# Two attention blocks on one core: block A's work two pieces earlier, a second place for output groups in two late units, and four small moves

## The chip, the cores and the metric

The program runs on one core of a Trainium2 chip. The core has TensorE (PE in the profile; its weight loads are listed as PEld), VectorE (DVE), ScalarE (ACT), GpSimd (POOL) and SyncE (SP), which here only issues DMAs, in program order on one queue. The metric is device time in microseconds (us); lower is better. A measurement is the median of several runs, and one more execution was taken with the profiler.

## The reference

Two independent attention blocks, A and B, each on its own input of 2048 rows x 640 columns with 32 heads of 20 columns; all in float32.

```
qkv = x @ wqkv                      # [S, 3, H, Dh]
A:  logits[s, w] = q[s] . k[s - 2 w] * Dh**-0.5   for w = 0..7 (masked where s - 2 w < 0)
    o = softmax(logits) over w, times v[s - 2 w]
B:  scores = q k^T * Dh**-0.5 ;  o = softmax(scores) v     # all 2048 keys
out = concat(o_A @ wo_A, o_B @ wo_B)
```

So A is a sliding window of eight keys with a step of two, and B is full attention with 32 heads.

## The kernel before, in words

Every projection splits each float32 operand into a rounded high part and a low remainder ("split") and adds three products (`PASSES`): 15 matmuls per output tile of 128 rows. A copy makes the high part and a subtraction the low part; which engines do it is set per call in `split` (L175; ACT and DVE unless `first` and `second` say otherwise).

**Stage 1 (L525 to L577)** projects q, k and v of block A for its first 12 tiles of 128 rows and stores them to DRAM (`qa_d`, `ka_d`, `va_d`). **Stage 2 (L612 to L651)** projects q and k of block B: five values of `m`, four column blocks `n`, two halves `j`, that is 40 groups, each of 15 matmuls with 512 columns, in turn over all eight PSUM banks (`all_banks`). Each result is stored to `kb_d` (m = 0, 2 and half of 4) or `qb_d`. In its last row `m == 8` it also starts the loads for B's attention: `b_keys(0)` returns four DMAs for the k stack of the first four heads (L586), `b_queries` four for each of four query blocks (L594).

**Stage 3 (L1021 to L1055)** projects v of block B: 30 of 32 groups (`v_group`, 15 matmuls with 320 columns, results on four PSUM banks). Between them it computes the first 24 steps of row maxima, `b_max(i)` (L753): four q.k matmuls into two pairs of banks (`wide`, which alternates between the two pairs), each pair read by one VectorE reduction of 128 x 1024. One `b_max` follows each group from the seventh on.

**Stage 4, the loop (L1091)**, has 512 steps in 32 units of 16. Each unit holds the attention of four heads for 512 queries: per step four score matmuls with the keys on partitions (`ss` two at once, or `sm` one of them beside one matmul for the maxima), four exponentials on ACT, four matmuls with v (`b_pv`, marked `P`), and 24 steps ahead the matmuls for the row maxima (`MM` or `sm`), which VectorE reduces. The order of a unit is written out by hand in three lists: `UNIT_V` (L877) for units 0 to 23, `UNIT` (L873) for units 24 to 29, and `PAIR` for the half unit 30 until the maxima end. Beside these, `V` stands for one group of A's remaining projections (tiles 12 to 15, `a_more`, L1004), and `G` for one group of A's output projection (`group`, L1083), which also lets VectorE's small operations run that have been collected in `beside`. In the last 60 steps `G` takes two output groups if they are ready. A small planner (`one`, `two`, `b_two`) picks the PSUM bank for each matmul from estimated end times.

**Block A's attention** runs on GpSimd as 128 pieces (`UNITS`, L348): for each tile four pieces of keys and four of values, each of two window positions. `a_fetch` loads a piece two pieces ahead, `a_attention` (L450) is a generator, and each `next(a_work)` emits one piece: 12 times in stage 2 (L649), 8 times in stage 3, then every fourth step of the loop from step 15. The softmax of a tile starts with its fourth piece of keys; its small VectorE operations wait for the next `G`, unless the tile is in `late`, when they are emitted at once (L403). The last tile has no keys of a following tile between its own keys and its values. A finished tile is transposed (`a_turn`, five VectorE transposes at a `G`, then a round trip through DRAM), split by GpSimd into `aot`, of which there is one buffer (`turn_parts`, L496), and used by two output groups of 15 matmuls.

**The end.** From step 488 on, steps run in pairs without maxima. Output rows of B are normalised on GpSimd, stored to `ot_b`, loaded back and split (`out_first` for four chunks, `out_last` for the fifth, L927), and multiplied by `wo_b` in groups of 15 matmuls.

SP, GpSimd, PE, ACT and DVE all keep program order: what is emitted ahead of an instruction runs ahead of it on that engine. Nearly all instructions are recorded under one line (L61), so the profile is read by tile names: `ve` is a v projection, `bk,bq` and `bq,bk` are q.k matmuls for maxima and scores, `mx` the maxima, `e` the exponentials, `e,vb` the matmuls with v, `more` and `braw` B's partial sums, `akv`, `al`, `am` and `ao` block A's work, `xl` the fifth chunk of split rows, `ww` split weights.

Of the kernel before, what the change touches and what calls it, by code (L numbers as in the profile page):

```python
# [40 lines left out]
NKB = 16  # L41
# [24 lines left out]
def attention_pair(ctx, tc, xa, wqk_a, wv_a, wo_a, xb, wqk_b, wv_b, wo_b, oa, ob):  # L66
# [108 lines left out]
    def split(hi, lo, src, tag="stg", second=None, first=None):  # L175

        t = sb.tile([128, 640 if tag == "stg" else 1024], F32, tag=tag, bufs=3 if tag == "stg" else PB, name="stg")
        raw = t[:, :src.free_size()] if len(src.shape) == 2 else (
            t[:, :src.shape[1] * src.shape[2]].rearrange("p (k c) -> p k c", c=src.shape[2]))
        sp.dma_start(raw, src)  # L180

        def parts():
            (first or act.copy)(hi, raw)
            (second or dve).tensor_tensor(lo, raw, hi.bitcast(F32), ALU.subtract)
        after(odd(wait[0]), parts)
# [167 lines left out]
    def a_fetch(n):  # L353
        if n >= len(UNITS):
            return
        t, c = UNITS[n]
        assert loop[0] is None or t < in_dram[0]
        hf, r0 = divmod(t * 128, HS)
        if c == 0:
            q = sb.tile([128, D], F32, tag="aq", bufs=2, name="aq")  # L360
            sp.dma_start(q, qa_d[hf, r0:r0 + 128])
            a_t[t] = [q, None, None]
        kv = sb.tile([128, 2, D], F32, tag="akv", bufs=4, name="akv")
        src = ka_d if c < 4 else va_d
        for o in range(2):
            r = r0 + 2 * (c % 4) + o
            sp.dma_start(kv[:, o], src[hf, r:r + 128])
        a_kv[n] = kv
# [217 lines left out]
    def b_keys(g):  # L586
        k = big(3 * (g % 2), [128, 2, S], "bk")
        v = sb.tile([128, NKB, VG], F32, tag="vb", bufs=2, name="vb")
        stacks[g] = (k, v)
        return [lambda r=r, r0=r0, s0=s0, n=n: sp.dma_start(  # L590
            k[r * HALF + r0:r * HALF + r0 + n].bitcast(F32), kb_d[s0:s0 + n, g * GH + 2 * r:g * GH + 2 * r + 2])
            for r in range(2) for r0, s0, n in BK_RUNS]
# [20 lines left out]
    for m in range(0, 10, 2):  # L613
        nxt = []
        for n in range(4):
            for j in range(2):
                p = next(banks)
                for k in range(KC):
                    for i, (wi, xi) in enumerate(PASSES):
                        pe.matmul(p, WB[j][:, wi, k], chunk(XB[n], xi, k), start=(k == 0 and i == 0),  # L620
                                  stop=(k == KC - 1 and i == 2))
                c = MS[m + j]
                o = (0, 1) if c < KC else (1, 0)
                pt = sb.tile([128, 2, 512], F32R, tag="p", bufs=PB, name="pr")
                act.copy(pt[:, o[0]], p)
                dve.tensor_tensor(pt[:, o[1]], p, pt[:, o[0]].bitcast(F32), ALU.subtract)
                after(1, sp.dma_start, dst_b(c, n).rearrange("t p c -> p t c"), pt.bitcast(F32))
                tick()
                if loads:
                    loads.pop(0)()  # L630
                if m < 8 and (n, j) in ((1, 0), (1, 1)):
                    w, loads = m_pieces(MS[m + 2 + len(nxt)])
                    nxt.append(w)
                elif m == 8 and (n, j) == (0, 1):
                    WV, loads = wide_pieces(wv_b[0])
                elif m == 8 and n == 3:
                    if j == 0:
                        wait[0] = 4
                        w1, more = wide_pieces(wv_b[1])
                        for fn in more:  # L640
                            fn()
                if m == 8 and n > 1:
                    if (n, j) == (2, 0):
                        k_loads = b_keys(0)
                        rings.append(big(1, [128, NQC, 2, 512], "bq"))
                        q_loads = [fn for qc in range(NQC) for fn in b_queries(0, qc)]
                    k_loads.pop(0)()
                groups += 1
                if 4 < groups < 34 and groups * 2 % 5 < 2:  # L649
                    next(a_work, None)  # L650
        WB = nxt  # L651
    tick()
# [183 lines left out]
    def b_two(what):  # L836
# [41 lines left out]
        "sm P sm MM ss P sm ss MM sm P ss MM sm P sm sm MM sm V sm ss MM sm P sm MM ss P sm MM sm ss P sm MM "  # L878
        "ss P sm MM sm ss P sm sm sm P sm ss MM ss G sm MM ss sm P sm MM ss P sm MM sm ss P sm sm sm P sm ss "
        "MM sm P sm MM ss P sm MM ss").split()  # L880
    SLOT = UNIT[:UNIT.index("G")].count("P") - 1

    def b_units(pv, group, more):

        scores = ((i, pl, r) for i in range(NS - LEAD) for pl in range(2) for r in range(2))
        maxima = ((m, j) for m in range(LEAD, NS) for j in range(2))
        steps = iter(range(-LAG, NS))
        half = []
        for i in range(0, NS - LEAD, NKB):
            for t in UNIT_V if i // NKB < 6 * (NT - UP) else UNIT if i + NKB <= NS - LEAD else PAIR * (NKB // 4):  # L890
                if t == "P":
                    yield
                    pv(next(steps))
                elif t == "G":
                    group()
                elif t == "V":
                    more()
                elif t == "ss":
                    b_two([("s", *next(scores)) for _ in range(2)])
                elif t == "MM":  # L900
                    m, j = next(maxima)
                    max_tiles(m)
                    b_two([("m", m, j, r) for r in range(2)])
                    max_end(m, 1)
                else:
                    s = next(scores)
                    shut = bool(half)
                    m, j, r = half.pop() if shut else (*next(maxima), 1 - s[2])
                    max_tiles(m)
                    if not shut:  # L910
                        half.append((m, j, 1 - r))
                    b_two([("s", *s), ("m", m, j, r)])
                    if shut:
                        max_end(m, 1)
# [12 lines left out]
    def out_last(qc):  # L927
        o = outs_b[qc]
        k = KC - 1
        split(chunk(o, 0, k), chunk(o, 1, k), ot_b[k * 128:(k + 1) * 128, qc * 512:(qc + 1) * 512])  # L930
        if qc < NQC - 1:
            for n in range(8):
                after(3 + (1 + (qc < 2)) * n, fill.append, lambda n=n: out_group(qc, n))
# [42 lines left out]

    rows_a = [(t + j, m) for t in range(UP, NT, 2) for m in range(6) for j in range(2)]
    xt, wt = {}, []
    in_dram = [UP]

    def a_columns(t):

# [20 lines left out]

    def a_more():  # L1004

        t, m = rows_a.pop(0)
        x, w = xt[t], wt[0]
        p = bank()
        rows15(p, lambda xi, k: chunk(x, xi, k), [w[:, 0], w[:, 1]])
        hf, r0 = divmod(t * 128, HS)  # L1010
        pad = PAD if m > 1 else 0
        store_rows(p, (qa_d, ka_d, va_d)[m // 2][hf, pad + r0:pad + r0 + 128, m % 2 * 320:m % 2 * 320 + 320])
        if m == 5:
            after(2, in_dram.__setitem__, 0, t + 1)
            if t + 2 < NT:
                after(12, a_columns, t + 2)
        if t % 2 and rows_a:
            for n, fn in enumerate(a_load()):
                after(2 + n, fn)
# [3 lines left out]
    for n, half, s in V_GROUPS[:-LAG]:  # L1023
        v_group(n, half, s)
        tick()
        groups += 1
        if q_loads:
            for _ in range(4 if groups == 1 else 1):
                q_loads.pop(0)()
        if groups == 1:  # L1030
            wait[0] = 5
        if groups in (8, 16):
            XB[groups // 8 - 1], more = x_pieces(xb, groups // 8 - 1, gp, (groups // 8 - 1, groups // 8 + 1))
            for fn in more:
                fn()
        if groups > 6:
            for i in islice(steps, 1):
                b_max(i)
        if groups in (9, 11, 15, 17, 19, 23, 25, 28):
            next(a_work, None)  # L1040
        if groups in (22, 23, 26):
            v_piece(0, *((8, 12), (12, 16), (0, 4))[(groups - 21) // 2])
        if groups in (18, 21):
            a_columns(UP + groups // 21)
        if groups == 24:
            for n, fn in enumerate(a_load()):
                after(2 + n, fn)
        if groups == 14:
            a_turn(*done_a.pop(0)[1:])
        turn_parts()  # L1050
        if groups == 28:
            wait[0] = 2
            load_out(wo_a, WO, (0,))
        if loads and groups >= 28:
            loads.pop(0)()  # L1055
# [129 lines left out]
```

## Time and profile before

| what | us |
|---|---|
| median of 3 runs | 1766.57 (1765.93 to 1769.04) |
| the profiled execution, its own time | 1765.34 |
| its span in the profile | 1763.5 |
| stage 1 (A's projections), to about | 160 |
| stage 2 (B's q and k), to about | 301 |
| stage 3 (B's v and the first maxima), to about | 402 |
| units 0 to 23 of the loop, to about | 1391 |
| units 24 to 29, to about | 1635 |

The profile gives for each engine its busy time, the idle time before an instruction and who ended it, all in us from the start of the span. The end of a unit is read from ACT's copy into `braw`, of which there is one per unit. An engine that is shown busy all the time need not be at its limit: matmuls overlap, and their ends are modelled.

### The profile page before, as it was taken

The page shows a single profiled execution, that of the slowest core. Times are in us where ns is not written, and L with a number is a line of the kernel's source. Part 1 is how long each engine was busy: PE and PEld are TensorE (multiplying, and loading weights), DVE is VectorE, ACT ScalarE, POOL GpSimd, SP SyncE. Part 2 cuts the span into 40 slices and gives each one's busy share as a digit, 9 for nine tenths or more (in the row PEclk, how much of TensorE's full clock was granted, in tenths as well). Part 3 has the DMA queues.
Part 4 walks back from the last instruction along what each step waited for, and adds up shares of the span by engine and source line. Part 5 has one row for each costly group of instructions (what it writes and reads, how often), then busy time and mean ns, then how long its engine had stood idle before and what let it go on. Part 6 is the DMA issues. An engine that isn't in the chain of part 4 may idle for free.

```text
span 1763.5 us, 31971 instructions
## 1 busy us (share of the span) xinstructions
PE 1749.7 (99%) x11331; PEld 998.7 (57%) x11331; DVE 1346.4 (76%) x1821; ACT 1333.1 (76%) x2598; POOL 1229.7 (70%) x1086
## 2 busy tenths in 40 slices
PE   9999999999999999999999999999999999999999
PEld 7988888874454444444444444444444444444569
DVE  3102333679999999999999999999999999999400
ACT  4323222229989999999999999989999999989981
POOL 0000683595888888888989888988888888745442
PEclk9999999999999999999999999999999999999999
DMA  7657868774536554644474456536552635222123
GB/s 260 194 172 241 301 240 268 239 233 118 158 100 172 142 163 127 152 134 135 154 172 138 133 150 157 160 100 177 140 159 91 144 109 143 62 73 63 57 72 114
DMA packets 212152, 269.74 MB, mean 153 GB/s; under 512 B 91676, under 2 KB 131740, under 8 KB 211000
## 3 DMA queue, kind: packets, MB, share of 16 engines
q1 hardware_dynamic: 211416, 267.04, 50.5%
q8 instruction: 89, 1.46, 0.3%
q10 hardware_dynamic: 576, 0.66, 0.1%
q14 instruction: 71, 0.58, 0.1%
HBM read 192.87 MB, written 74.74 MB: 152 GB/s over the span
## 4 chain that ended last, share of the span: by engine, by line
PE 88%; DVE 6%; POOL 2%; DMA 1%; issue 1%; ACT 1%; SPq 0%; DVEq 0%; POOLq 0%; ACTq 0%
PE ps_st L61 88%; DVE mx L61 6%; POOL akv L61 1%; DMA bk<-kb_d 1%; ACT e L61 1%; POOL xn L61 0%; DMA vb_d<-ve 0%; SPq L61 0%; POOL ww L61 0%; POOL braw L61 0%; DMA stg<-xa 0%; POOL ao L61 0%; DMA rb<-s_d 0%; POOL xl L61 0%; POOL aot L61 0%
## 5 line engine op out<-in xcount | busy, mean ns | idle before, releaser
L61 DVE TENSOR_REDUCE mx<-ps_st 128x1 f32<-128x512 f32 (+1 forms) x1500 | 1219.3, 879 | 76.0 <-PE ps_st L61 66.2
L61 ACT ACTIVATE e<-ps_st 128x512 f32<-128x512 f32 x2048 | 1067.3, 608 | 36.3 <-PE ps_st L61 17.8
L61 PE MATMUL ps_st<-bq,bk 62*128 62x512 f32 x2048 | 610.3, 440 | 0.8 <-DVE mx L61 0.6
L61 PEld LDWEIGHTS ps_st<-bq,bk 62*128 62x128 f32 x2048 | 288.4, 184 | 479.0 <-ACT e L61 351.9
L61 PE MATMUL ps_st<-bk,bq 60*128 60x512 f32 x2048 | 555.4, 433 | 2.6 <-DVE mx L61 1.8
L61 PE MATMUL ps_st<-e,vb 128*32 128x512 f32 x4096 | 542.9, 604 | 3.2
L61 POOL TENSOR_TENSOR braw<-braw,more 128x512 f32<-128x512 f32 x224 | 287.9, 1285 | 147.3 <-ACT more L61 137.2
L61 POOL TENSOR_TENSOR akv<-akv,aq 128x1280 f32<-128x1280 f32 x64 | 188.5, 2946 | 184.7 <-DMA akv<-ka_d 184.7
L61 POOL TENSOR_TENSOR akv<-akv 128x640 f32<-128x640 f32 (+3 forms) x304 | 282.7, 930 | 23.8
L61 PEld LDWEIGHTS ps_st<-bk,bq 60*128 60x128 f32 x2048 | 269.4, 184 | 34.0 <-DVE mx L61 12.5
L61 ACT COPY ro<-ps_st 128x320 f32<-128x320 f32 (+2 forms) x132 | 62.6, 476 | 192.2 <-PE ps_st L61 160.0
L61 PEld LDWEIGHTS ps_st<-e,vb 128*32 128x32 f32 x4096 | 82.0, 108 | 158.9 <-issue 72.4
L61 POOL TENSOR_TENSOR akv<-akv,al 128x1280 f32<-128x1280 f32 x64 | 151.9, 2374 | 0.2
L61 ACT COPY more<-ps_st 128x512 f32<-128x512 f32 x224 | 132.5, 592 | 1.6 <-PE ps_st L61 1.4
L61 PE MATMUL ps_st<-ww,xn 128*128 128x320 f32 x768 | 125.8, 314 | 0.0
L61 PEld LDWEIGHTS ps_st<-ww,xn 128*128 128x128 f32 x768 | 113.6, 188 | 19.7 <-ACT e L61 8.4
L61 PE MATMUL ps_st<-xn,w 128*128 128x512 f32 x480 | 117.6, 393 | 0.0
L61 PEld LDWEIGHTS ps_st<-xn,w 128*128 128x128 f32 x480 | 90.1, 188 | 21.0
L61 ACT CAST pr<-ps_st 128x512 fp32r<-128x512 f32 x40 | 23.6, 589 | 103.5 <-PE ps_st L61 103.5
L61 PE MATMUL ps_st<-wc,xn 128*128 128x512 f32 (+1 forms) x432 | 101.5, 380 | 0.1
L61 DVE TENSOR_TENSOR pr<-ps_st,pr 128x512 fp32r<-128x512 f32 x40 | 27.7, 692 | 93.0 <-ACT pr L61 90.2
L61 PEld LDWEIGHTS ps_st<-wc,xn 128*128 128x128 f32 x432 | 80.3, 189 | 14.2 <-ACT xn L61 0.5
(71 smaller groups left out, 1065.7 us busy)
## 6 DMA issues: line engine op xcount, KB each, us to landing
akv<-ka_d SPq DMA_DIRECT2D x128, 320.0 KB
akv<-va_d SPq DMA_DIRECT2D x128, 320.0 KB
wx<-wa_d SPq DMA_DIRECT2D x24, 480.0 KB
kb_d<-pr SPq DMA_DIRECT2D x20, 512.0 KB
qb_d<-pr SPq DMA_DIRECT2D x20, 512.0 KB
bk<-kb_d SPq DMA_DIRECT2D x16, 640.0 KB
bq<-qb_d SPq DMA_DIRECT2D x64, 160.0 KB
rb<-s_d SPq DMA_DIRECT2D x128, 64.0 KB
```

The costliest lines, as they stand in the source:

```text
L61: return self.tc.keep_in_program_order(op(*a, **k))
```

## The change

Six edits, in the order of the code.

```diff
-        assert loop[0] is None or t < in_dram[0]
+        assert loop[0] is None or t < in_dram[c >= 4]
...
-                if m == 8 and n > 1:
+                if m == 8 and n:
+                    if (n, j) == (1, 0):
+                        first_loads = b_keys(0)
                     if (n, j) == (2, 0):
-                        k_loads = b_keys(0)
                         rings.append(big(1, [128, NQC, 2, 512], "bq"))
                         q_loads = [fn for qc in range(NQC) for fn in b_queries(0, qc)]
-                    k_loads.pop(0)()
+                        first_loads += [q_loads.pop(0) for _ in range(2)]
+                    first_loads.pop(0)()
                 groups += 1
-                if 4 < groups < 34 and groups * 2 % 5 < 2:
+                if 2 < groups < 36 and groups * 2 % 5 < 2:
                     next(a_work, None)
...
+    UNIT_0 = ["P", "sm"] + UNIT_V[2:]
...
-            for t in UNIT_V if i // NKB < 6 * (NT - UP) else UNIT if i + NKB <= NS - LEAD else PAIR * (NKB // 4):
+            for t in UNIT_0 if not i else UNIT_V if i // NKB < 6 * (NT - UP) or i // NKB in (28, 29) else UNIT if i + NKB <= NS - LEAD else PAIR * (NKB // 4):
...
-        split(chunk(o, 0, k), chunk(o, 1, k), ot_b[k * 128:(k + 1) * 128, qc * 512:(qc + 1) * 512])
+        by = () if qc else ("stg", gp, gp.tensor_copy)
+        split(chunk(o, 0, k), chunk(o, 1, k), ot_b[k * 128:(k + 1) * 128, qc * 512:(qc + 1) * 512], *by)
...
-    in_dram = [UP]
+    in_dram = [UP, UP]
...
     def a_more():
+        if not rows_a:
+            out_piece()
+            return
...
+        if m in (3, 5):
+            after(2, in_dram.__setitem__, m // 4, t + 1)
         if m == 5:
-            after(2, in_dram.__setitem__, 0, t + 1)
...
-            for _ in range(4 if groups == 1 else 1):
+            for _ in range(2 if groups == 1 else 1):
                 q_loads.pop(0)()
...
-        if groups > 6:
-            for i in islice(steps, 1):
+        if groups > 7:
+            for i in islice(steps, 1 + (groups == 12)):
                 b_max(i)
```

- The k stack's four loads are emitted at the third to sixth group of the row `m == 8` instead of the fifth to eighth; two of the sixteen query loads follow at the seventh and eighth, and stage 3 begins with two of them instead of four.
- Stage 2 emits 14 pieces of A's attention instead of 12, at groups 3 and 35 beside the old places, so every later piece is emitted two places earlier. The note of which rows are in DRAM is kept for keys and values apart, since the keys of a late tile are now fetched before its values are computed.
- The first `b_max` follows the eighth group of stage 3 instead of the seventh, and the twelfth group is followed by two.
- Unit 0 begins with `P` and then one `sm`, where they were the other way round.
- Units 28 and 29 use `UNIT_V`; as A's projections are done by then, its `V` takes one of A's output groups, if one is ready.
- The fifth chunk of B's first 512 finished rows (`out_last(0)`) is split by GpSimd alone.

## The prediction, made before the changed kernel was run

> **What bounds the kernel now.** I read the page first, for the busy shares and the chain that ended last:
>
> ```profile
> PE 1749.7 (99%) x11331; PEld 998.7 (57%) x11331; DVE 1346.4 (76%) x1821; ACT 1333.1 (76%) x2598; POOL 1229.7 (70%) x1086
> PE 88%; DVE 6%; POOL 2%; DMA 1%; issue 1%; ACT 1%; SPq 0%; DVEq 0%; POOLq 0%; ACTq 0%
> ```
>
> PE is shown busy nearly always and holds 88% of the chain, DVE 6%. The shares mix stages, so the next view is a table of windows: stage 2, stage 3, and units 0 to 23. Columns: window and length, then the busy us of PE, PEld, DVE, ACT and POOL, the clock, the DMA share, GB/s.
>
> ```profile
> 160.00:301.00 141.00, 141.00 (x611) 114.36 (x610) 46.93 (x60) 35.49 (x59) 85.67 (x74) 1.00 0.77 266
> 301.00:402.00 101.00, 98.77 (x622) 81.00 (x620) 69.65 (x72) 27.43 (x56) 66.92 (x56) 1.00 0.76 236
> 402.00:1391.00 989.00, 984.32 (x6862) 470.33 (x6858) 947.47 (x1306) 911.72 (x1787) 851.25 (x748) 1.00 0.50 142
> ```
>
> Stages 2 and 3 are PE's: DVE and ACT have room, and only stage 3 shows 2.2 us without a matmul. In the loop PE, DVE (96%) and ACT (92%) are all nearly full, so a gain there must remove a wait between them. One V unit takes 989.00 / 24 = 41.21 us. The same view, cut at the copies into `braw`, gives units 24, 25, 26, 28 and 29:
>
> ```profile
> 1391.63:1431.39 39.76, 39.55 (x273) 16.88 (x275) 38.62 (x51) 37.34 (x75) 33.88 (x27) 1.00 0.65 157
> 1431.39:1470.92 39.53, 39.50 (x273) 17.13 (x275) 39.25 (x56) 37.17 (x75) 37.72 (x37) 1.00 0.44 124
> 1470.92:1511.55 40.63, 40.23 (x273) 17.36 (x274) 38.80 (x52) 37.58 (x76) 34.23 (x28) 1.00 0.33 102
> ...
> 1551.10:1592.97 41.87, 41.69 (x288) 19.29 (x289) 39.02 (x55) 37.62 (x75) 20.20 (x20) 1.00 0.24 65
> 1592.97:1634.84 41.87, 41.70 (x288) 19.35 (x288) 38.06 (x50) 37.62 (x75) 22.69 (x24) 1.00 0.25 75
> ```
>
> Units with one output group take 39.5 to 39.8 us with DVE at 97 to 99%: DVE sets them. Unit 26 has about 1 us more for the same work. Units 28 and 29 hold two output groups in one `G` (288 matmuls instead of 273) and take 41.87; DVE has room in them.
>
> **The change, part by part.**
>
> *Stage 2.* Two calls for A (the first, with the 7 loads of three pieces, at group 3 instead of 5, and one with 2 loads at group 35) and the k stack's loads go earlier on SP's queue, past two weight loads, B's stores and `wv_b`. I cost this at nothing: PE is busy 141.00 of 141.00 us. If a weight arrived some microseconds later, ACT would wait for it with the copies behind it, but the 40 results rotate over eight banks, so PE has seven groups, over 20 us at 141.00 / 40 = 3.5 us each, before it lacks one. The price without that cover: seven loads of 320 KB are 2.3 MB, 8.6 us at the 266 GB/s of the first row; I keep none of it in the sum. GpSimd starts A's work some 7 us earlier. The two notes of rows in DRAM emit nothing.
>
> *First k stack.* The chain shows the stack's last load late; PE's timeline shows the first `b_max`, and an undisturbed one further on:
>
> ```profile
> 303.15 12.18 DMA bk<-kb_d
> ```
>
> ```profile
> 316.68 0.50 PE L61 MATMUL ps_st<-bk,bq 60*128 60x512 f32 x1
> 317.59 0.70 PE L61 MATMUL ps_st<-bk,bq 60*128 60x512 f32 x3 [0.41 <-DMA vb_d<-ve]
> 318.22 2.02 PE L61 MATMUL ps_st<-ww,xn 128*128 128x320 f32 x12
> ...
> 338.98 0.73 PE L61 MATMUL ps_st<-bk,bq 60*128 60x512 f32 x4
> 339.64 2.03 PE L61 MATMUL ps_st<-ww,xn 128*128 128x320 f32 x12
> ```
>
> The first costs 318.22 - 316.68 = 1.54, the other 339.64 - 338.98 = 0.66. The loads come two groups (7 us) earlier and are needed one group later, so the 0.88 us goes. Bounds: 0 and -0.9; I take **-0.9**.
>
> *Maxima elsewhere.* One `b_max` moves from group 7 to group 12. Two in a row need four pairs of banks where there are two, so the third pair of matmuls waits for the first VectorE reduction and the fourth for the second. The nearest rows are DVE's, and PE's a little later, where DVE was late:
>
> ```profile
> 339.52 2.36 DVE L61 TENSOR_REDUCE mx<-ps_st 128x2 f32<-128x1024 f32 x2 [0.71 <-PE ps_st L61]
> ...
> 368.61 2.34 DVE L61 TENSOR_REDUCE mx<-ps_st 128x2 f32<-128x1024 f32 x2
> ```
>
> ```profile
> 369.87 0.49 PE L61 MATMUL ps_st<-bk,bq 60*128 60x512 f32 x2 [0.28 <-DVE mx L61]
> 371.00 0.50 PE L61 MATMUL ps_st<-bk,bq 60*128 60x512 f32 x2 [0.64 <-DVE mx L61]
> 371.44 2.03 PE L61 MATMUL ps_st<-ww,xn 128*128 128x320 f32 x12
> ```
>
> DVE starts 339.52 - 338.98 = 0.54 after the first matmul, each reduction takes 1.18, and PE follows an end by some 0.05 (368.61 + 2.34 = 370.95, then 371.00). So the fourth pair starts 0.54 + 2.36 + 0.05 = 2.95 after the first and the next group 0.44 later (371.44 - 371.00), at 3.39 instead of 0.66: 2.73, of which 0.66 is only moved from group 7. Behind the waiting matmul are all of PE's later groups. DVE is caught up by the `b_max` after group 13, as a group (2.4) lies between. **+2.1**; bounds 0 (the wait replaces another one) and +2.7.
>
> *Unit 0.* The planner starts with all banks free, but the last `b_max` is still being read; the `sm` in front waits for it:
>
> ```profile
> 389.67 0.39 PE L61 MATMUL ps_st<-bq,bk 62*128 62x512 f32 x1
> 390.92 0.49 PE L61 MATMUL ps_st<-bk,bq 60*128 60x512 f32 x1 [0.86 <-DVE mx L61]
> 391.35 2.02 PE L61 MATMUL ps_st<-ww,xn 128*128 128x320 f32 x12
> ...
> 394.79 2.02 PE L61 MATMUL ps_st<-ww,xn 128*128 128x320 f32 x12
> ```
>
> From 389.67 to 394.79 are one group (2.40) and four pairs; at 0.33 a pair (half of 0.66) that would be 3.7, so 1.4 us is waiting, 0.86 of it marked. With the group first, DVE is done reading before the `sm` comes. Late next are the exponentials, which start a group later, for the first `b_pv`. I take **-1.15**, between the marked and the whole wait; bounds 0 and -1.4.
>
> *A two pieces ahead.* In the loop every piece keeps its place in the four-step rhythm, but the softmax's small DVE operations fall on the other unit of each pair; over 24 units that only swaps odd and even. GpSimd is busy 851 of 989 us, so its order costs nothing while it keeps up. What changes is the last tile's softmax, forced out in unit 26 (ACT, POOL, DVE rows):
>
> ```profile
> 1501.34 0.42 ACT L61 ACTIVATE al<-al 128x256 f32<-128x256 f32 x1
> ```
>
> ```profile
> 1501.84 0.45 POOL L61 TENSOR_TENSOR am<-al 128x128 f32<-128x128 f32 x1 [1.37 <-ACT al L61]
> ```
>
> ```profile
> 1503.05 0.35 DVE L61 RECIPROCAL am<-am 128x32 f32<-128x32 f32 x1 [0.80 <-POOL am L61]
> ```
>
> In one step ACT's exponential, GpSimd's sums and DVE's reciprocal follow each other, and DVE waits 0.80. Counting steps: the tile's last keys are called at step 411 now and 403 after; its maximum then goes at the `G` of step 409 instead of 425, the sums at step 419, and the forced reciprocal at 423 finds them ready. Unit 26 then costs what 24 or 25 do: 40.63 less 39.53 to 39.76, **-1.0**; bounds 0 and -1.1.
>
> *Units 28 and 29.* The last two tiles, both groups at the `G` of steps 457 and 473, now go one to `V` and one to `G`. For that a tile must be ready at step 451: the transposed tile 14 now comes at step 433 and waits for tile 13's second group at 441, its split is emitted at 442 and released seven steps later, 449. Tile 15 likewise: 465 for step 467. The same matmuls run; the unit becomes a V unit, 41.21 instead of 41.87: **-1.3**. Bounds: 0, and -5.3 if only DVE counted (rival 1).
>
> *`out_last(0)`.* It stands where DVE has no gap (DVE, then PE, then POOL rows):
>
> ```profile
> 1613.49 26.58 DVE L61 TENSOR_REDUCE mx<-ps_st 128x1 f32<-128x512 f32 x32 [3.63 <-PE ps_st L61]
> 1640.11 0.69 DVE L61 TENSOR_TENSOR xl<-stg,xl 128x512 fp32r<-128x512 f32 x1
> ```
>
> ```profile
> 1647.35 1.69 PE L61 MATMUL ps_st<-bq,bk 62*128 62x512 f32 x8 [0.63 <-DVE mx L61]
> ```
>
> ```profile
> 1631.23 0.61 POOL L61 CAST xn<-stg 128x512 fp32r<-128x512 f32 x1
> 1631.93 1.28 POOL L61 TENSOR_TENSOR xn<-stg,xn 128x512 fp32r<-128x512 f32 x1
> ...
> 1645.64 1.28 POOL L61 TENSOR_TENSOR braw<-braw,more 128x512 f32<-128x512 f32 x1 [0.84 <-ACT more L61]
> ```
>
> DVE loses 0.69, and PE waits for DVE at the end of the stretch: **-0.6**; bounds 0 and -0.7. GpSimd gets 0.61 + 1.28 = 1.9 us; it idles 0.84 before the add at 1645.64, so the rest could delay that add by 1 us, and nothing of B's output needs it at once. Without that slack the first output group would start late by at most 1.9.
>
> **Sum**: -0.9 + 2.1 - 1.15 - 1.0 - 1.3 - 0.6 = -2.85 us. The profiled execution took 1765.34, so the changed one should take 1762.5. The median of the runs is 1.23 above the profiled execution; with that, the forecast is **1763.7**, 0.16% below 1766.57.
>
> **Rivals.**
>
> 1. *PE is not at its limit in units 28 and 29*, and they fall to DVE's work: 38.06 us at the 97% of unit 24, 39.2, that is 2.7 a unit instead of 0.65. Total -2.85 - 4.0 = -6.9: 1759.7. Against it: V units also hold two groups apart, and take 41.21 with DVE 4% idle. [...] Chance 0.08.
> 2. *The doubled `b_max` costs nothing*, because PE would have waited at that place anyway, for a bank or for data moved with the loads: -4.95, so 1761.6. Against it: PE has no idle time around group 12. Chance 0.20.
> 3. *GpSimd comes late in the loop* (slower). `aot` has one buffer, and its split now stands right behind the `G` that reads it for the last time. If GpSimd is ahead there, it waits for PE with B's adds behind it; once those are late, ACT finds no free `more`, and PE stops. Twelve tiles in V units at what one late step cost in unit 26, 1.0, are +12: 1775.7. It decides from about 0.55 us a tile. For it: GpSimd is 86% busy. Against: it has 11 us to spare in two units. Chance 0.08.
> 4. *The change doesn't do what it says*: tile 14 misses step 451 and both its groups still share a `G` (+0.65), and the stack is still late (+0.9): -1.3, so 1765.3. Chance 0.14.
>
> **How the numbers follow.** The forecast has 0.50; its own terms leave it between 1762.3 and 1766. A measurement of this kernel can tell about 0.2%, 3.5 us, from no change, so the bounds are 1763.04 and 1770.1. I put 0.14 of the forecast's 0.50 below 1763.04; with rivals 1 and 2 that is faster 0.42. Slower is rival 3, 0.08; the rest, 0.50, is no difference. The range, 1760.9 to 1766.8, leaves out rivals 1 and 3 and a little of each tail.
>
> **What would show it.** The first `b_max` at 0.66 with no wait; two PE waits at the double one, together some 2 us; no wait of DVE at the start of unit 0; unit 26 below 39.9; units 28 and 29 at 41.0 to 41.4 with one group of 15 matmuls in each place; no `xl` on DVE before 1650. The forecast is wrong if units 0 to 23 together change by over 1 us, or if the doubled `b_max` shows no wait.

## The result, and the profile after

The changed kernel took 1771.95 us (median of 8 runs, 1771.31 to 1773.72) against 1766.25 for the kernel before (8 runs): the ratio is 1.0032, 95% interval 1.0023 to 1.0041. It is slower by 5.7 us, where 2.85 less was forecast. Its profiled execution took 1773.72 us with a span of 1771.9. This was the slowest of its eight runs, so a second profile of the same kernel was taken later (experiment 11 below: 1770.62 us, span 1768.8). Both are used.

From the page after, the busy shares and the chain that ended last. PE still holds 87%, DVE has grown from 6 to 8, and DMA from 1 to 2:

```profile
PE 1753.7 (99%) x11331; PEld 1001.1 (56%) x11331; DVE 1348.8 (76%) x1824; ACT 1333.3 (75%) x2597; POOL 1233.0 (70%) x1088
PE 87%; DVE 8%; DMA 2%; ACT 1%; issue 1%; POOL 0%; SPq 0%; DVEq 0%; POOLq 0%; ACTq 0%
```

The windows of the kernel after, with the cuts of the prediction for the stages (columns as there; the third number from the end is the clock):

```profile
160.00:301.00 141.00, 141.00 (x610) 114.27 (x610) 48.19 (x59) 35.38 (x59) 100.31 (x89) 1.00 0.81 273
301.00:402.00 101.00, 94.65 (x554) 79.17 (x553) 62.69 (x64) 20.62 (x42) 56.35 (x45) 0.93 0.74 225
402.00:1391.00 989.00, 984.48 (x6855) 470.28 (x6854) 946.13 (x1305) 908.82 (x1781) 851.70 (x746) 1.00 0.50 143
```

The reader is to see two things in the second row: PE is 6.35 us idle where it was 2.23, and the granted clock is 0.93 where it was 1.00. Stage 2 is as full as before and the loop has hardly moved. The same view, cut at the copies into `braw`, for units 26, 28 and 29:

```profile
1480.97:1520.72 39.75, 39.65 (x273) 17.24 (x274) 39.20 (x56) 37.15 (x75) 32.41 (x24) 1.00 0.30 82
...
1560.52:1602.16 41.64, 41.39 (x290) 19.58 (x290) 39.02 (x52) 38.15 (x75) 20.29 (x20) 1.00 0.19 52
1602.16:1643.56 41.40, 41.18 (x288) 19.35 (x284) 38.34 (x52) 37.94 (x74) 22.14 (x23) 1.00 0.27 74
```

The copies into `braw` cut each span into five stretches (us; the last column is the sum, the span):

| profile | to the first `braw` | units 0 to 23 | 24 to 27 | 28, 29 | to the end | span |
|---|---|---|---|---|---|---|
| before | 401.50 | 990.13 | 159.47 | 83.74 | 128.66 | 1763.5 |
| after, first | 411.25 | 990.45 | 158.82 | 83.04 | 128.34 | 1771.9 |
| after, second | 406.39 | 990.63 | 158.85 | 83.06 | 129.87 | 1768.8 |

So the late units gained 1.3 us, and nearly all the loss lies ahead of the loop: 9.75 us in the first profile and 4.89 in the second, which loses 1.2 more at the end. The first place is the start of stage 3. The chain of waits of the kernel after, in that stretch (start, length, what):

```profile
288.99 10.36 DMA stg<-wv_b
...
299.37 0.74 ACT ww L61
...
302.00 11.41 DMA stg<-wv_b
...
313.43 0.73 ACT ww L61
```

SP's queue of the kernel before, and then of the kernel after, shows what stands beside these loads:

```profile
289.15 0.46 SPq L61 DMA_DIRECT2D stg<-wv_b  x1
...
292.64 0.46 SPq L61 DMA_DIRECT2D stg<-wv_b  x1
293.20 0.81 SPq L61 DMA_DIRECT2D bk<-kb_d  x1
...
299.23 0.36 SPq L61 DMA_DIRECT2D qb_d<-pr  x1
299.65 1.92 SPq L61 DMA_DIRECT2D stg<-wv_b  x3
```

```profile
286.14 0.80 SPq L61 DMA_DIRECT2D bk<-kb_d  x1
287.04 0.81 SPq L61 DMA_DIRECT2D akv<-ka_d  x2
...
288.99 0.56 SPq L61 DMA_DIRECT2D stg<-wv_b  x1
289.60 0.73 SPq L61 DMA_DIRECT2D bk<-kb_d  x1
...
301.58 0.37 SPq L61 DMA_DIRECT2D qb_d<-pr  x1
302.00 2.37 SPq L61 DMA_DIRECT2D stg<-wv_b  x3
```

Before, the first `bk` load is issued behind three of the `wv_b` loads. After, two `bk` loads and the two loads of one piece of A come ahead of or right behind the second one, which then takes 10.36 us. ACT waits for it and makes its copies of results late; the store of a result (`qb_d<-pr`) is late with them, at 301.58 instead of 299.23; and the last three `wv_b` loads, which stand behind that store on SP, are issued at 302.00 instead of 299.65 and take 11.41 us. What holds them so long once they are issued is not shown by itself. The two query loads that were moved too are issued behind them, the first at 304.41. What waits for them, on ACT (the line of the waits between 284 and 330 us: total, times, longest) and on PE:

```profile
ACT ww L61 <- DMA stg<-wv_b: 13.5, 4, 6.3
```

```profile
314.21 3.89 PE L61 MATMUL ps_st<-ww,xn 128*128 128x320 f32 x12 [3.12 <-ACT ww L61]
317.90 1.00 PE L61 MATMUL ps_st<-ww,xl 128*128 128x320 f32 x3
```

The same weights and the start of the same group in the kernel before, on ACT and on PE:

```profile
306.29 2.00 ACT L61 CAST ww<-stg 128x640 fp32r<-128x640 f32 x3
```

```profile
309.99 1.92 PE L61 MATMUL ps_st<-ww,xn 128*128 128x320 f32 x12
```

PE waits 3.12 us for the weights of the fifth v group, and the group then takes 3.89 + 1.00 instead of 1.92 + 0.60. The granted clock tells why (windows of 2 us of the kernel after, the last one of 6 us):

```profile
312.00:314.00 2.00, 0.00 (x0) 0.00 (x0) 0.00 (x0) 0.57 (x1) 0.00 (x0) 0.97 0.73 275
314.00:316.00 2.00, 1.79 (x5) 1.43 (x6) 1.81 (x3) 1.76 (x5) 0.00 (x0) 0.50 0.75 269
316.00:318.00 2.00, 2.00 (x9) 2.00 (x9) 0.21 (x1) 0.23 (x1) 0.00 (x0) 0.50 0.69 234
318.00:320.00 2.00, 2.00 (x9) 2.00 (x8) 0.00 (x0) 0.43 (x1) 0.00 (x0) 0.50 0.63 215
320.00:322.00 2.00, 2.00 (x13) 2.00 (x13) 0.00 (x0) 0.00 (x0) 0.00 (x0) 0.82 0.57 175
...
340.00:342.00 2.00, 1.00 (x4) 0.47 (x4) 2.00 (x3) 0.00 (x0) 0.17 (x1) 0.80 0.79 285
342.00:348.00 6.00, 6.00 (x22) 4.80 (x21) 2.34 (x3) 1.32 (x3) 0.00 (x0) 0.50 0.03 9
```

No window here is below 0.50. If the clock is either 1.00 or 0.50 (an assumption; windows wholly inside a fall read 0.50, those outside 1.00), a window of 2 us at 0.97 holds (1 - 0.97) / 0.5 x 2 = 0.12 us at half clock. So the five rows of the first fall hold 0.12 + 2 + 2 + 2 + 0.72 = 6.84 us of it, and PE, whose twelve matmuls at half clock take 3.89 us for 1.92, loses half of that by this estimate, 3.4 us. The clock falls a second time, for 6.8 us (0.8 and 6), behind the doubled `b_max`. Its two waits come as forecast, 1.72 us together where the forecast had some 2 (PE of the kernel after):

```profile
338.55 0.74 PE L61 MATMUL ps_st<-bk,bq 60*128 60x512 f32 x4
340.37 0.50 PE L61 MATMUL ps_st<-bk,bq 60*128 60x512 f32 x2 [1.09 <-DVE mx L61]
341.50 0.80 PE L61 MATMUL ps_st<-bk,bq 60*128 60x512 f32 x2 [0.63 <-DVE mx L61]
342.23 3.57 PE L61 MATMUL ps_st<-ww,xn 128*128 128x320 f32 x12
```

In the second profile of the same kernel the wait for the weights is the same, and so are the two at the doubled `b_max`, but no fall of the clock follows the latter, and the one at the weights is shorter, 0.28 + 2 + 1.12 = 3.40 us (PE, then windows):

```profile
313.32 0.60 PE L61 MATMUL ps_st<-ww,xn 128*128 128x320 f32 x2 [3.12 <-ACT ww L61]
...
338.27 0.49 PE L61 MATMUL ps_st<-bk,bq 60*128 60x512 f32 x2 [1.09 <-DVE mx L61]
339.40 0.50 PE L61 MATMUL ps_st<-bk,bq 60*128 60x512 f32 x2 [0.64 <-DVE mx L61]
```

```profile
312.00:314.00 2.00, 0.60 (x2) 0.30 (x2) 0.70 (x1) 1.33 (x2) 0.00 (x0) 0.93 0.65 237
314.00:316.00 2.00, 1.82 (x7) 1.82 (x8) 1.35 (x3) 1.13 (x4) 0.00 (x0) 0.50 0.80 308
316.00:318.00 2.00, 2.00 (x12) 2.00 (x12) 0.00 (x0) 0.24 (x1) 0.00 (x0) 0.72 0.77 282
...
340.00:342.00 2.00, 2.00 (x14) 2.00 (x15) 1.61 (x2) 0.00 (x0) 0.00 (x0) 1.00 0.00 0
342.00:344.00 2.00, 2.00 (x14) 1.45 (x13) 1.22 (x2) 1.61 (x3) 0.16 (x1) 1.00 0.16 58
...
1652.00:1654.00 2.00, 2.00 (x12) 1.15 (x16) 0.30 (x2) 1.21 (x3) 1.46 (x3) 0.50 0.02 2
```

Its clock falls once more, for 3.44 us, at 1652 where the maxima end. So the falls take 6.8 us from the first profile and 3.4 from the second, which is the difference of their spans (3.1) nearly; without them, the kernel after would be some 1.6 to 1.9 us over the one before, whose profile has no fall. At the end of the maxima PE waits longer than before (0.63), in both profiles of the kernel after; the first has this row:

```profile
1656.52 1.20 PE L61 MATMUL ps_st<-bq,bk 62*128 62x512 f32 x8 [1.83 <-DVE mx L61]
```

### The profile page after: what moved, and what is told of

Same layout as the page of the kernel before. It is cut to its first block, busy times and chain, and to the rows that moved or that the text cites. A ratio compares the mean times of both kernels' runs of the same rounds, so it can differ in the third digit from the quotient of the medians.

```text
span 1771.9 us, 31988 instructions
## 1 busy us (share of the span) xinstructions
PE 1753.7 (99%) x11331; PEld 1001.1 (56%) x11331; DVE 1348.8 (76%) x1824; ACT 1333.3 (75%) x2597; POOL 1233.0 (70%) x1088
## 4 chain that ended last, share of the span: by engine, by line
PE 87%; DVE 8%; DMA 2%; ACT 1%; issue 1%; POOL 0%; SPq 0%; DVEq 0%; POOLq 0%; ACTq 0%
PE ps_st L61 87%; DVE mx L61 8%; DMA stg<-wv_b 1%; ACT e L61 1%; DMA stg<-wo_a 1%; POOL akv L61 0%; POOL ww L61 0%; DVE mtr L61 0%; ACT more L61 0%; POOL ao L61 0%; ACT ww L61 0%; DVE pr L61 0%; POOL braw L61 0%; SPq L61 0%; POOL al L61 0%
## 5 line engine op out<-in xcount | busy, mean ns | idle before, releaser
L61 PE MATMUL ps_st<-ww,xn 128*128 128x320 f32 x768 | 130.3, 321 | 3.1 <-ACT ww L61 3.1
L61 PEld LDWEIGHTS ps_st<-ww,xn 128*128 128x128 f32 x768 | 117.6, 194 | 23.7 <-ACT e L61 9.6
```

Source lines behind the costliest of these rows:

```text
L61: return self.tc.keep_in_program_order(op(*a, **k))
```

## The experiments

The first theory: the k stack's loads, put between the loads of `wv_b`, make the split weights late, and that wait with the fall of the clock behind it is the loss. Rivals: A's two more calls in stage 2 make them late; or the doubled `b_max` is the loss. Where a ratio is given, it is against the kernel before, measured beside it; its 95% interval reaches some 0.001 (1.7 us) to either side, in the last two runs nearly 0.002.

**1. The k stack's and the first query loads in their old places**, all else as changed:

```diff
-                if m == 8 and n:
-                    if (n, j) == (1, 0):
-                        first_loads = b_keys(0)
+                if m == 8 and n > 1:
                     if (n, j) == (2, 0):
+                        k_loads = b_keys(0)
...
-            for _ in range(2 if groups == 1 else 1):
+            for _ in range(4 if groups == 1 else 1):
```

> The changed kernel with the loads of the first k stack (and two of the query loads) back in their old place behind the weights of the v projection. Theory (the stack's loads are ahead of the v weights on the one queue and make these late): PE's waits of 0.60 and 3.12 us for split weights at 303 and 314 us go, and with them the half clock that follows from 314 to 320; stage 3 reaches its last maxima 6 to 8 us earlier than in the changed kernel's trace, and the time falls to 1764.5 to 1767.5. Rival (the two extra pieces of block A in stage 2 make the weights late): the waits stay, the time stays at 1770 to 1773.

Measured: 1766.74 us, ratio 1.0 (0.9991 to 1.0009). ACT's wait for `wv_b` is gone, in this kernel's waits:

```profile
ACT ww L61 <- DMA stg<-wv_b: 0.2, 1, 0.2
```

PE has no wait of that kind left, and the first `braw` comes at 403.86. The median lies 5.2 us below that of the changed kernel, nearly the whole of its loss.

**2. A's two more calls of stage 2 taken back**, the k loads left early:

```diff
-                if 2 < groups < 36 and groups * 2 % 5 < 2:
+                if 4 < groups < 34 and groups * 2 % 5 < 2:
```

> The changed kernel with block A's pieces in their old places (12 in stage 2). Theory (the k stack's loads make the v weights late): the waits of 3 us or more for split weights stay, and unit 26 has its extra 0.9 us again and units 28 and 29 the double G: 1771 to 1774. Rival (the extra pieces make them late): the waits go, 1765 to 1768.

Measured: 1771.11 us, 1.0028 (1.0018 to 1.0037). PE still waits for the weights, 2.35 + 0.30 us. So the k loads alone make them late, and A's two calls make this wait 1.1 us longer (0.60 + 3.12 against 2.35 + 0.30). The median lies only 0.8 below that of the changed kernel, but that is a net figure: units 26, 28 and 29 take 40.63, 43.03 and 42.72, as without the two pieces ahead `V` finds no output group and `G` holds two, and units 24 to 29 together take 3.6 us more than in the changed kernel. So what A's earlier pieces gain there, they lose elsewhere, in longer waits and falls of the clock; the runs do not say how much in each.

**3. The first maxima in their old places** (no doubled `b_max`):

```diff
-        if groups > 7:
-            for i in islice(steps, 1 + (groups == 12)):
+        if groups > 6:
+            for i in islice(steps, 1):
```

> The changed kernel with the first maxima back in their old places, one after each group from the seventh. Theory (the doubled maxima cost their two waits, 1.7 us together, and then some 3 us more because the granted clock falls to half behind them): the time between the first and the last maxima of stage 3 is shorter by about 4.9 us less the one that is moved, no clock under 1.0 after 330 us, and the median falls by 3 to 5 us to 1767 to 1769. Rival (only the waits count, and the clock falls for another reason): 2.1 us, 1769.5 to 1770.5, with the fall of the clock still there.

Measured: 1770.44 us, 1.0018 (1.0008 to 1.0027). The profiled execution had the first `braw` at 405.64, 5.6 us before the first profile of after, but the median fell by only 1.5: this was the first sign that the first profile of after was not a typical run. The median is in the rival's range, but the fall of the clock that the rival kept is not there: the only one in this profile ahead of its last 4 us is at the weights.

**4. The extra `b_max` as two halves**, after groups 12 and 16:

```diff
-            for i in islice(steps, 1 + (groups == 12)):
-                b_max(i)
+            for i, j in islice(steps, 2 + (groups in (12, 16))):
+                b_max(i, j)
...
```

> The changed kernel with the extra maxima spread: half a step more (one pair of banks) after group 12 and after group 16. Theory (the clock falls when PE waits twice within 3 us, 1.7 us in all; a single wait of 1.1 us is too short for it): two single waits of about 1.1 us, no half clock, 2 to 3 us less than the changed kernel in its profile, median 1769 to 1770.5. Rival (any wait of about 1 us brings the clock down): two falls of the clock, time as the changed kernel or above, 1771.5 to 1775.

Measured: 1772.88 us, 1.003 (1.0021 to 1.004); a miss. Each half still waits 1.09 us, so two places with one wait each took the place of one with two (1.09 and 0.63):

```profile
338.72 0.51 PE L61 MATMUL ps_st<-bk,bq 60*128 60x512 f32 x2 [1.09 <-DVE mx L61]
352.56 0.51 PE L61 MATMUL ps_st<-bk,bq 60*128 60x512 f32 x2 [1.09 <-DVE mx L61]
```

The clock stayed at 1.00 behind both, and the profiled execution took 1769.84, 3 us less than the median; see 12.

**5. Both the k loads and the first maxima as before**, the rest (unit 0, A ahead, units 28 and 29, `out_last(0)`) as changed; the edits of 1 and 3 together.

> The changed kernel with both the first k stack's loads and the first maxima in their old places; block A ahead, unit 0, units 28 and 29 and the split of the fifth chunk by GpSimd stay. Theory (the loads and the doubled maxima are all of the loss, the four other edits gain what the changed kernel's trace shows from the last maxima of stage 3 on: 1.5 in unit 0, 0.65 in units 24 to 27, 0.7 in units 28 and 29, 0.3 after them): 1762 to 1764.5, no wait over 1 us in stage 3. Rival (the other edits gain nothing once every run is counted, as the wait at the end of the maxima grew from 0.63 to 1.83 us and brings the clock down in some runs): 1765 to 1767.

Measured: 1765.09 us, 0.9991 (0.9981 to 1.0001). That is the rival's range: the four other edits gained less than the trace had promised. With the runs above, all four combinations of the two edits have been measured. Against the kernel before beside each, the medians are +5.7 (both moved), +4.0 (k loads moved), +0.3 (maxima moved) and -1.5 (neither): the k loads cost 5.4 to 5.6, the maxima 1.7 to 1.9, and the two add up as far as the intervals can tell.

**6. As 5, and `out_last(0)` split by ACT and DVE again:**

```diff
-        by = () if qc else ("stg", gp, gp.tensor_copy)
+        by = ()
```

> As the run before, and the fifth chunk of the first finished rows split by ACT and VectorE again. Theory A (moving that split away from VectorE changes the banks that the planner gives to the last maxima, and this makes PE wait 1.83 us for the last reduction instead of 0.63): the wait is 0.6 to 0.8 us again, the clock stays at 1.0 after 1640 us, and the median is 0 to 1.5 us below the run with the split on GpSimd. Theory B (the order in units 28 and 29 makes the longer wait): the wait stays at 1.8 us, and the median is 0.6 us above.

Measured: 1767.04 us, 0.9995 (0.9985 to 1.0005), 1.95 above run 5, though the two intervals overlap. From the last `braw` to the matmul that waits at the end of the maxima it took 14.04 us (1635.95 to 1649.99) against 12.96 in run 5 (1634.98 to 1647.94). The wait itself stays 1.84, so the split on GpSimd does not make it: theory A is refuted.

**7. The kernel before with the moved maxima alone** (the edit of 3 the other way round).

> The kernel before with only the first maxima moved (first after the eighth group, two after the twelfth). Theory (the two waits of 1.7 us are followed by half a clock for some us): the first maxima no longer wait (0.9 us less), the double costs 2.1 us and 1 to 3 us more behind it at a lower clock: median 1.5 to 4 us above the kernel before. Rival (the waits alone): 1.2 us above it, clock 1.0 throughout.

Measured: 1767.95 us, 1.0005 (0.9995 to 1.0014). The runs fall into groups: 1765.88 to 1766.18 at a mean clock of 0.999 to 1.0, 1767.83 to 1768.98 at 0.999, 1770.35 and 1770.78 at 0.998. The waits (1.09 and 0.63) are there; the profiled execution, of the first group, has no fall of the clock behind them. The median lies 1.3 above the kernel before, close to the rival's 1.2, but not with the clock at 1.0 throughout in every run.

**8. As 5, and at step 488 the planner's free banks sorted by the time at which they are read**, so that the bank that VectorE reads last is taken last:

```diff
+        if read_at:
+            free.sort(key=lambda n: read_at[n])
+            pair[0] += max(read_at[4:6]) < max(read_at[6:])
         read_at.clear()
```

> The run with the first k stack and the first maxima in their old places, and one line more: where the planned banks end (step 488), the free banks are taken in the order in which the planner expects them to be read, instead of 3, 0, 1, 2 (bank 3 is read last there). Theory (the 1.83 us wait at the end of the maxima is for the bank that is read last, and the clock falls behind it in some runs): the first matmul there waits under 0.7 us, the clock stays at 1.0 after 1640 us, 1 to 3 us less than without the line: 1762.5 to 1764.5. Rival (PE needs all the banks at once there): the wait only moves to a later matmul, 1764.5 to 1766.

Measured: 1763.75 us, 0.9987 (0.9978 to 0.9997); the gain over run 5 is within the intervals. The wait of 1.83 is down to 0.41, and yet the clock falls behind it in this profile (PE's row, then windows of 2 us):

```profile
1644.40 2.29 PE L61 MATMUL ps_st<-bq,bk 62*128 62x512 f32 x8 [0.41 <-ACT e L61]
```

```profile
1646.00:1648.00 2.00, 2.00 (x11) 0.51 (x14) 0.23 (x2) 2.00 (x5) 1.53 (x3) 0.56 0.02 2
1648.00:1650.00 2.00, 2.00 (x13) 0.24 (x5) 0.00 (x0) 1.25 (x3) 0.16 (x1) 0.58 0.05 6
```

**9. As 8, with the first `b_max` after the eighth group again, and the extra one as halves in the middle of groups 12 and 16**, so that VectorE has time between the pairs (the line that places them):

```diff
+        v_group(n, half, s, (lambda: b_max(*next(steps))) if groups in (11, 15) else None)
...
```

> As the run before, but with the maxima starting after the eighth group, and the extra step spread as two halves in the middle of groups 12 and 16, where the banks have been read by then. Theory (a matmul for the maxima that finds its bank free costs only its own time, and the k stack in its old place is in time for the eighth group): no wait over 0.6 us from 300 to 370 us, none for the k stack or the queries, clock 1.0; 0.5 to 2 us below the run before, 1761.5 to 1763.5. Rival (VectorE is too far behind by then): a wait of about 1 us after each of the two groups, and no gain.

Measured: 1762.84 us, 0.9982 (0.9973 to 0.9991): ahead of both kernels, and 0.9 below run 8, which is within the intervals. No wait stands at the extra halves, the wait at the end of the maxima is 0.41, and the clock stays full up to the last 2 us of the span, as in these two windows (at the second of the halves, and behind that wait):

```profile
340.00:344.00 4.00, 4.00 (x28) 3.24 (x26) 4.00 (x9) 0.43 (x1) 4.00 (x3) 1.00 0.59 192
...
1648.00:1652.00 4.00, 4.00 (x31) 2.98 (x23) 0.00 (x0) 2.89 (x7) 1.58 (x2) 1.00 0.03 3
```

**10. As 5, and units 28 and 29 in their old order:**

```diff
-            for t in UNIT_0 if not i else UNIT_V if i // NKB < 6 * (NT - UP) or i // NKB in (28, 29) else UNIT ...
+            for t in UNIT_0 if not i else UNIT_V if i // NKB < 6 * (NT - UP) else UNIT ...
```

> The run with the first k stack and the first maxima in their old places, and units 28 and 29 in their old order, with both output groups at the G. Theory (the order of units 28 and 29 saves 0.3 to 0.5 us in each and makes the 1.2 us longer wait at the end of the maxima): the units take 41.9 us, the wait is 0.6 us, the clock stays at 1.0 there; the median is the same or up to 1 us lower than with the new order. Rival (the wait comes from block A's earlier pieces): the wait stays at 1.8 us and the median is about 1 us higher.

Measured: 1764.91 us, 0.999 (0.9981 to 0.9999), level with run 5. The units take 41.89 and 41.86 again, and the wait at the end of the maxima is the old one:

```profile
1647.34 1.69 PE L61 MATMUL ps_st<-bq,bk 62*128 62x512 f32 x8 [0.63 <-DVE mx L61]
```

**11 and 12. The changed kernel and kernel 4 once more, unchanged, for a second profile each.**

> The changed kernel itself, unchanged, with a second profile. Its first profile was the slowest of its 8 runs (1773.72 us, granted clock 0.996) and had half clock at 314 to 320 us (after a wait of 3.12 us) and at 342 to 348 us (after 1.09 + 0.63 us). Theory 1, the waits alone decide: the same waits (3.1 at 314, 1.09 + 0.63 near 340) and the same two falls of the clock, the span within 1 us of 1771.9. Theory 2, the fall after a wait varies from run to run: the same waits within 0.2 us, but a fall at only some of the places (the 3.1 us one surely, the doubled maxima perhaps not), and a span some 2 to 3 us per missing fall shorter. The median in either case 1771 to 1773.

> The kernel e4 (extra maxima as two halves) itself, with a second profile. Its first profile, 1769.84 us, was 3 us faster than its median of 1772.88 and had half clock only after the weight wait, none after the single waits of 1.09 us at 338.7 and 352.6. Theory 1, the waits alone decide: the same picture again, and the median stays unexplained. Theory 2, it varies from run to run: if this profile comes out near 1772 to 1774 us, it has the same waits and one or two more falls of the clock, at 339 or 353 or near 1650. The median 1771.5 to 1774.

Measured: 1772.09 us, 1.0027 (1.0011 to 1.0043), and 1772.29 us, 1.0031 (1.0013 to 1.0049). The waits of over 1 us are within 0.3 us of those of the first profiles, the falls of the clock are not at the same places; so it is theory 2 that the changed kernel's second profile bears out. Kernel 4's second profile (1771.09 us) again shows 1.00 behind both waits of 1.09, but half clock at the end of the maxima, where its first profile had none. The mean clock of the runs says the rest: 0.999 in the first profile, 0.997 in six of that kernel's ten runs, and 0.002 of 1770 us is 3.5, about the 3 us by which its median lies above that profile. So run 4 most likely missed by falls of the clock, in places that its first profile does not show.

## Why the prediction was wrong, step by step

- **Stage 2 at nothing: this step failed.** The prediction named the danger, a weight some microseconds late with ACT's copies behind it, and covered it with the eight banks of results. In the two profiles of the changed kernel stage 2 is indeed still full (141.00 of 141.00 us busy). But a bank holds a result; no bank stands in for a weight that a group needs to start. The prediction named `wv_b` among the loads that are passed, and then looked only at stage 2: `wv_b` is split by the same ACT for stage 3, whose fifth group uses it at once. The trace of before shows how little room that group had: its weights are cast at 306.29 (ACT, no wait), and it starts at 309.99. Runs 1 and 2 put the cause on the k loads, run 5 the price: 5.4 to 5.6 us against the -0.9 that the early loads were to bring. "The price without that cover" (8.6 us) came near that size by luck: it counts A's seven loads at group 3 and none of the four k loads.
- **The same step, in stage 2 itself**: A's call at group 3 makes stage 2's own weights late as well. ACT waits 5.5 to 7.2 us for them, near 190 us, in all eleven profiles with A's pieces ahead, and not at all in the three without (before, runs 2 and 7). In the changed kernel's two profiles there was just room for that; in seven of the eleven PE waited too. From its first matmul to the first v group, stage 2 took 138.86 us in the kernel before, 138.87 in the first profile of after, and 139.5 to 140.9 in those seven. In run 5's profile this is 1.5 us, one reason why it gained less than its theory said. The rows of run 1, ACT's and PE's:

```profile
189.80 0.72 ACT L61 CAST w<-stg 128x640 fp32r<-128x640 f32 x1 [6.26 <-DMA stg<-wqk_b]
```

```profile
190.58 0.74 PE L61 MATMUL ps_st<-xn,w 128*128 128x512 f32 x2 [0.65 <-ACT w L61]
```

- **First k stack**: its own gain came. The first `b_max` has no wait, 0.73 to 0.74 us for 0.66 to the next group.
- **Maxima elsewhere**: right in mechanism and size, as far as waiting goes. The forecast was two waits of some 2 us together and 2.1 in all; the waits are 1.09 + 0.63 = 1.72. In the second profile two `b_max` lie 5.79 apart (336.45 to 342.24) around the double one, where one group and one `b_max` take 3.06 and the moved one 0.66: 2.07. In the first profile the same place costs 4.9 up to the end of the slow stretch, as the clock fell. The medians say 1.7 to 1.9 (run 5). Rival 2, no wait, is refuted.
- **Unit 0**: -1.49 in the first profile and -1.47 in the second (from the last `b_max` of stage 3 to the first `braw`), a little beyond the whole of the wait, for -1.15.
- **Unit 26**: 40.63 to 39.75, -0.88 for -1.0; the other three units of that row change by up to 0.25. Right. Units 0 to 23 lost 0.3 to 0.5, within the mark of 1 us that was set for rival 3; GpSimd was not late. So neither of the two signs showed that the prediction set for itself as proof of being wrong: the loss came where it had set none.
- **Units 28 and 29**: half the size, -0.7 for -1.3: 41.64 and 41.40, not 41.21. And a cost that no term had: by the new order the matmul behind the maxima waits 1.83 instead of 0.63 for VectorE, because the planner takes first the bank that is read last (runs 6, 8 and 10). That is +1.2, so the edit is worth nothing that runs 5 and 10 can show (1765.09 and 1764.91). Rival 1 is refuted: DVE has 2.6 to 3 us to spare in both units and they still take 41.64 and 41.40.
- **`out_last(0)`**: -1.08 in the traces of runs 5 and 6, for -0.6. Run 10, which has this edit and the old wait of 0.63, takes 127.5 us from the end of unit 29 where the kernel before takes 128.7, so there it is not lost again.

The sum of the first profile, by these steps: the first `b_max` comes at 326.31 where the kernel before would have had it, one group on, at 320.62 - 1.54 = 319.08: +7.2; the first stack -0.9; the doubled `b_max` +4.9; unit 0 -1.5; units 0 to 23 +0.3; 24 to 27 -0.65; 28 and 29 -0.7; the end -0.3: +8.4, the difference of the spans. In the second: +5.1 (324.21) - 0.9 + 2.1 - 1.5 + 0.5 - 0.6 - 0.7 + 1.2 = +5.2, of 5.3, close to the medians' +5.7. By cause instead of place, 3.4 of these 5.3 us are half clock, which no term had, and 1.9 the waits less the gains.

## What to carry to other kernels

Before loads are moved ahead on a queue, look for the tightest load behind them, in the next stage too, and read its slack from its own consumer (here 306.29 against 309.99), not from the share of busy time of the stage in which they are issued. A wait of TensorE must be priced with what the clock does behind it (here half clock takes 6.8 us from the first profile of the changed kernel and 3.4 from the second), and one profile isn't enough for that: take a second one if its time is at the edge of the runs. A reorder that shifts the last user of a bank shifts the wait at the end of the stretch as well; here, taking the free banks in another order cut that wait by 1.4 us (1.83 to 0.41, runs 5 and 8), twice the 0.7 that the reorder gained in its two units.

## What the runs showed of the hardware

The granted clock fell to 0.50 behind some waits of PE, and in these profiles it did so in two lengths: worked out from windows of 2 us as above, every fall ahead of the last 4 us of a span, 16 in 14 profiles, held 3.40 to 3.44 us of half clock (13 of them) or 6.80 to 6.84 (three), by the same estimate a loss of 1.7 or 3.4 us. Behind the waits for weights (2.35 to 3.19 us) it fell in all six profiles that have one; behind 1.83 us at the end of the maxima in five of eight; behind 1.09 and 0.63 close together in two of five; behind a single 1.09 in none of four; and behind waits of 0.41 to 0.64 at the end of the maxima in two of six, once (run 8) with 0.41 us shown; the one fall left (run 6, at 320) follows two waits for DMAs at the first `b_max`, 0.84 and 0.73, where run 5 with 0.94 and 0.51 has none. So half clock came more often behind the longer of these waits (6 of 6, 5 of 8, then 4 of 15 at 1.09 us and below), but no length seen below 2.35 us decides, and the same kernel with the same waits has falls at other places in another run.

What sets the two lengths is not shown. In run 8 3.44 us of half clock followed a wait of 0.41. Why it did so there and not behind the 0.41 of run 9, and where the falls lie in runs without a profile, stays open.
